# The sixth expert's rows by quarter gathers and VectorE, and a smaller margin in the plan of the searches

## The chip, the cores and the metric

The kernel runs on one core of one Trainium2 chip. Its engines are TensorE (PE, with its weight loads as PEld), VectorE (DVE), ScalarE (ACT), GpSimd (POOL), which issues gathers, scatters and accumulating transfers here, and SyncE (SP), which issues the plain loads. The metric is the time of one execution on the device in microseconds; lower is better.

## The reference

The input is first put through an attention with decay (8 batches of 8 heads, 576 positions of 64 values): scores are scaled, multiplied by a decay that falls with the distance, and used without a softmax. Its output, 4608 rows of 512 values, goes to eight experts of two layers. The rows are shared out by a greedy rule over all gate values at once:

```python
logits = x @ w_gate                      # 4608 rows, 8 experts
order = np.argsort(-logits.flatten())
for idx in order:
    tok, e = (int(idx) // E, int(idx) % E)
    if assigned[tok] >= 0 or counts[e] >= cap:   # cap = 576
        continue
    assigned[tok] = e
    counts[e] += 1
...
for e in range(E):
    mask = assigned == e
    h = np.maximum(x[mask] @ w1[e], 0.0)         # 512 -> 1024
    out[mask] = h @ w2[e]                        # 1024 -> 512
```

Each expert ends up with exactly 576 rows.

## The kernel before

The attention comes first and leaves its rows in DRAM (`xd`), with the gate values in SBUF. Then the experts are computed one after another, in the order in which they fill up. Their numbers here are places in that order, from 0; the sixth is expert 5.

**The two layers.** An expert's 576 rows stand in five tiles of 128 (the last has 64). Every product is made in two parts, a high part rounded to a narrower format and the low rest, so that three matmuls stand for one: high by high, low by high, high by low. `l1` (line 1066) runs 16 groups of 12 matmuls into PSUM, in columns of 256 and 320; `l2` (line 1109) runs four tiles of 24 matmuls, in triplets, and the half tile of 16, in pairs. Weights come in 512 KB pieces by SP into four `raw` buffers; `conv` makes a piece's high part on ScalarE (line 955) and its low part in one of two ways: for `e < PIECES` by a negated copy on ScalarE (line 964) and an accumulating transfer that GpSimd issues (line 965), for the others by subtractions on VectorE (line 958).

**The rows of an expert.** For `e < PIECES`, five gathers of 128 rows (line 998), then in `transposes` four TensorE transposes for each of the five tiles (line 1030), a copy by ScalarE and a subtraction by VectorE (lines 1032 and 1033). For the others, 18 quarter gathers of 128 x 128 values (line 986), five stream transposes on VectorE into `xz` (line 1014), a copy by ScalarE (line 1016) and a subtraction by VectorE (line 1017). The weights of layer 1 are then read from an array with another order of rows (`in_w1n`), since the quarters place the values otherwise.

**The searches.** Which rows belong to the next expert is found while the present one is computed. `search` takes seven steps. In each, VectorE builds a table `G` (line 179), TensorE counts with nine small matmuls (line 355), and VectorE goes from the sums (`cs`, line 359) over a few tiny operations to the next digit. `members` follows (a scan into `sc`, line 414, `sm`, line 418, two small matmuls, lines 423 and 424, then lines 426 and 427), and then `listing`, which makes the list of row numbers: VectorE tables (lines 436 to 455), nine matmuls (line 461), for most experts one more (line 464), and the sums (line 469 on). For `p >= PIECES` the listing makes the quarters' numbers too (lines 478 to 482). `leave` takes the expert out of the choice.

**What sets the order.** Each engine runs its instructions in the order in which the program writes them, and waits by semaphores. The searches are generators that yield an assumed VectorE time and a TensorE time. `Mixer` keeps an assumed clock for TensorE (`t`, moved on by `adv` behind the layers' matmuls) and one for VectorE (`v`); a step's TensorE part is written behind the first layer matmuls at which `t` has reached `v + 150`, where `v` had the step's VectorE time times `slack` added:

```python
d, s.pe = next(s.side)
s.vec(d * s.slack)
s.ready = s.v + 150
...
while not hold and s.side is not None and s.ready <= s.t:
    s.step()
```

So the plan decides how many layer matmuls stand between two steps, and the hardware waits where the plan was too tight. Gathers are written as soon as a list is ready, quarter gathers 1300 ns of assumed time apart, and the transposes of an expert when `t` has passed an assumed arrival (`state['arrives']`).

Of the kernel before, what the change touches and what calls it, by code (L numbers as in the profile page):

```python
# [19 lines left out]
NP, HP, NB = 4, 4, 9  # L20
N, DM, E, FF = 4608, 512, 8, 1024
SLACK = 1.0
PIECES = 6

def consts_np():
    h = np.arange(H); g = (1.0 - 2.0 ** (-5.0 - h)).astype(np.float64)
# [61 lines left out]
class Route:  # L88
# [341 lines left out]
    def listing(s, p):  # L430
# [43 lines left out]
        if early:  # L474
            s.room(cn)
        if p >= PIECES:
            s.quarter = pool.tile([128, 20], I32, name="quarter", bufs=2)
# [423 lines left out]
def moe(tc, nc, P, R, xd, w1_d, w2_d, out, mix):  # L901
# [11 lines left out]

    def phases():
        for p in range(E):
            mix.slack = 1.0 if p < 2 else 1.2 if p < 4 else 1.35
            if p < E - 1:
                yield from (R.search() if p else R.search_first())
                regs[p] = nc.sync.value_load(R.e[0:1, 0:1], min_val=0, max_val=E - 1)
            state['listing'] = p  # L920
            yield from R.members(p)
            if p == E - 1:
                regs[p] = nc.sync.value_load(R.e[0:1, 0:1], min_val=0, max_val=E - 1)
            yield from R.listing(p)
            found.append(R.idx)
            if p >= PIECES:
                quarters[p] = R.quarter
            if p == 0:
                yield 0, 0
            if p < E - 1:  # L930
                yield from R.leave(p)

    def dma_pump():

        while state['dma'] < min(state['conv'] + 4, 8*E):
            e, k = divmod(state['dma'], 8)
            if e not in regs or state['dma'] >= state['most']:
                return
            t = P['raw']()
            src = ((w1_d[0] if e < PIECES else w1_d[1]) if k < 4 else w2_d)  # L940
            nc.sync.dma_start(t, src[bass.ds(regs[e], 1), :, (k % 4)*1024:(k % 4)*1024+1024].rearrange("a p x -> (a p) x"))
            RAW[e, k] = t
            state['dma'] += 1

    def conv(fast=False):

        e, k = divmod(state['conv'], 8)
        if state['dma'] <= state['conv']:
            mix.drain(lambda: e in regs)
            dma_pump()  # L950
        raw = RAW.pop((e, k))
        nm = "w1" if k < 4 else "w2"
        hi = P['w'].tile([128, 1024], F32R, name=nm + "h", bufs=4)
        lo = P['w'].tile([128, 1024], F32R, name=nm + "l", bufs=4)
        A.activation(hi, raw, AF.Copy)
        if e >= PIECES:
            for x in (slice(0, 512), slice(512, 1024)):
                V.tensor_tensor(lo[:, x], raw[:, x], hi[:, x].bitcast(F32), op=ALU.subtract)
                mix.vec(690)
        elif fast:  # L960
            for x in (slice(0, 512), slice(512, 1024)):
                lows.append(lambda x=x: V.tensor_tensor(lo[:, x], raw[:, x], hi[:, x].bitcast(F32), op=ALU.subtract))
        else:
            A.activation(lo, raw, AF.Copy, scale=-1.0)  # L964
            add = lambda: nc.gpsimd.dma_start(lo, raw, accum_op=ALU.add)  # L965
            if ready(0) and 0 not in XG:
                lows.append(add)
            else:
                add()
        (W1 if k < 4 else W2)[e, k % 4] = (hi, lo)  # L970
        state['conv'] += 1
        dma_pump()

    def gather(e, all=False):
        if e in XG or not ready(e):
            return
        if e >= PIECES:
            if e not in parts:
# [24 lines left out]
    def transposes(e):  # L1003
# [4 lines left out]
        XH[e], XL[e] = xh, xl  # L1008
        if e >= PIECES:
            low = []  # L1010
# [26 lines left out]
    def l1(e, tr):  # L1037
# [5 lines left out]
        for i, (f, s) in enumerate(order):  # L1043
# [36 lines left out]
            if i in ((2, 4, 7, 10) if e else (5, 7, 9, 11, 13)):  # L1080
                conv()
# [10 lines left out]
    def l2(e, hb):  # L1092
# [4 lines left out]
        for t in range(5) if e + 1 < E else (4, 0, 1, 2, 3):  # L1097
# [4 lines left out]
            for f in range(8):  # L1102
                wh, wl = [w[:, (f % 2)*512:(f % 2)*512+512] for w in W2[e, f // 2]]

                h = hb[:, f]
                for a, w in ((h[:, c], wh), (h[:, 640+128*t:768+128*t], wh), (h[:, c], wl)) if t < 4 else \
                        ((h[:, 512:640], wh), (h[:, c], wl)):
                    m = a.shape[1]
                    T.matmul(ps[:m], a, w, start=(k == 0), stop=(k == last), skip_group_check=True)  # L1109
                    k += 1  # L1110
                mix.adv(650)
                gather(e + 1)
                wait -= 1

                soon = state['listing'] == e + 1 and not ready(e + 1)
                if want and wait <= 0 and e + 1 in regs and not soon:
                    conv()
                    want, wait = want - 1, 6
                if late and not soon:
                    late.pop(0)()  # L1120
                if e + 1 in XG and e + 1 not in XH and mix.t > state['arrives']:
                    tr = transposes(e + 1)
                next(tr, None)
# [9 lines left out]
        for _ in range(want):  # L1133
            conv()
# [6 lines left out]
    def prepare():  # L1141
# [4 lines left out]
                                     in_offset=bass.IndirectOffsetOnAxis(ap=z[:, 0:1], axis=0))  # L1146

    mix.start(phases())

    def run():  # L1150
# [98 lines left out]
```

## Time and profile before

| what | value |
|---|---|
| three runs | 619.55, 617.11, 616.14 us, median 617.11 |
| profiled execution | 619.8 us, of it the span of the instructions 618.0 us |
| granted TensorE clock, mean over the span | 0.989 |
| PE busy | 596.2 us (96%) |
| PEld busy | 517.8 us (84%) |
| DVE busy | 431.5 us (70%) |
| ACT busy | 252.0 us (41%) |
| POOL busy | 244.1 us (39%) |

A share of busy time is a mean over the whole span. TensorE is the engine that is nearly always busy; where it isn't, the timeline tells in brackets how long it stood before an instruction and which engine released it. In such a row the first number is the start in us from the beginning of the span, the second the busy time, then come engine, line, operation, written and read tiles, shape and number of instructions. The start of the next row of the same engine tells what an instruction costs when others follow, since matmuls overlap.

### The profile page before, as it was taken

The page shows a single profiled execution, that of the slowest core. Times are in us where ns is not written, and L with a number is a line of the kernel's source. Part 1 is how long each engine was busy: PE and PEld are TensorE (multiplying, and loading weights), DVE is VectorE, ACT ScalarE, POOL GpSimd, SP SyncE. Part 2 cuts the span into 40 slices and gives each one's busy share as a digit, 9 for nine tenths or more (in the row PEclk, how much of TensorE's full clock was granted, in tenths as well). Part 3 has the DMA queues.
Part 4 walks back from the last instruction along what each step waited for, and adds up shares of the span by engine and source line. Part 5 has one row for each costly group of instructions (what it writes and reads, how often), then busy time and mean ns, then how long its engine had stood idle before and what let it go on. Part 6 is the DMA issues. An engine that isn't in the chain of part 4 may idle for free.

```text
span 618.0 us, 14880 instructions
## 1 busy us (share of the span) xinstructions
PE 596.2 (96%) x5768; PEld 517.8 (84%) x5768; DVE 431.5 (70%) x1511; ACT 252.0 (41%) x437; POOL 244.1 (39%) x313
## 2 busy tenths in 40 slices
PE   8899997998999999999999999999999999999995
PEld 5788786876599889888987998898889789989983
DVE  6747886988889888878885976688578665544400
ACT  2334332333455446453562555166335234433310
POOL 5787635504512261262242143223314658711011
PEclk9999997998999999999999999999999999999998
DMA  9999999864688599696988398569928743440010
GB/s 329 407 379 398 278 329 334 278 168 154 185 234 171 178 232 251 194 213 200 200 220 266 70 248 207 176 142 242 249 82 186 207 158 116 152 142 27 0 43 34
DMA packets 51224, 124.83 MB, mean 202 GB/s; under 512 B 7186, under 2 KB 22418, under 8 KB 51154
## 3 DMA queue, kind: packets, MB, share of 16 engines
q1 hardware_dynamic: 37906, 80.10, 37.3%
q0 software_dynamic: 13104, 43.53, 31.2%
q8 instruction: 45, 0.74, 0.5%
q10 hardware_dynamic: 144, 0.26, 0.1%
q14 instruction: 25, 0.20, 0.1%
HBM read 80.35 MB, written 18.87 MB: 161 GB/s over the span
## 4 chain that ended last, share of the span: by engine, by line
PE 72%; issue 11%; DMA 8%; DVE 4%; POOL 3%; SPq 0%; POOLq 0%; ACT 0%; DVEq 0%
PE ph L1066 29%; PE py L1109 25%; DMA vin<-in_vk 4%; PE sc L605 3%; PE px L649 3%; DMA xd<-raw 3%; PE pS L626 2%; PE r L355 2%; PE px L640 2%; PE pt L1030 2%; POOL out_y L1086 1%; PE warm L1201 1%; PE r L461 1%; DMA qin<-in_qk 1%; PE pT L681 1%
## 5 line engine op out<-in xcount | busy, mean ns | idle before, releaser
L1109 PE MATMUL py<-w2h,hb 128*128 128x512 f32 x576 | 187.3, 397 | 0.1
L1066 PE MATMUL ph<-xh,w1h 128*128 128x320 f32 (+1 forms) x512 | 151.9, 301 | 0.2 <-ACT xh L1032 0.2
L1066 PE MATMUL ph<-xl,w1h 128*128 128x320 f32 (+1 forms) x512 | 149.2, 296 | 0.0
L1066 PE MATMUL ph<-xh,w1l 128*128 128x320 f32 (+1 forms) x512 | 149.0, 296 | 0.0
L1109 PE MATMUL py<-w2l,hb 128*128 128x512 f32 (+1 forms) x320 | 125.3, 391 | 0.1
L1109 PEld LDWEIGHTS py<-w2h,hb 128*128 128x128 f32 x576 | 104.5, 188 | 21.9 <-issue 0.3
L1066 PEld LDWEIGHTS ph<-xh,w1h 128*128 128x128 f32 x512 | 96.0, 189 | 1.3 <-ACT xh L1032 0.7
L1066 PEld LDWEIGHTS ph<-xl,w1h 128*128 128x128 f32 x512 | 96.2, 190 | 0.3
L1066 PEld LDWEIGHTS ph<-xh,w1l 128*128 128x128 f32 x512 | 96.0, 189 | 0.0
L1070 ACT ACTIVATE hb<-ph 128x256 fp32r<-128x256 f32 (+1 forms) x128 | 51.9, 408 | 105.2 <-PE ph L1066 98.9
L1086 POOL DMA_INDIRECT out_y<-yt,idx x40 | 40.3, 1008 | 129.4 <-ACT yt L1126 72.8
L1075 DVE SCALAR_TENSOR_TENSOR hb<-ph,hb 128x256 fp32r<-128x256 f32 (+1 forms) x192 | 57.7, 350 | 28.6 <-ACT hb L1070 24.3
L1109 PEld LDWEIGHTS py<-w2l,hb 128*128 128x128 f32 (+1 forms) x320 | 56.7, 177 | 13.5 <-issue 0.5
L590 POOL TENSOR_TENSOR qin<-qin,cst 128x512 f32<-128x512 f32 (+1 forms) x48 | 47.0, 1005 | 42.6 <-DMA qin<-in_qk 38.6
L1126 ACT ACTIVATE yt<-py 128x512 f32<-128x512 f32 x32 | 19.1, 597 | 98.2 <-PE py L1109 65.3
L629 ACT ACTIVATE st<-pS,cst 128x128 f32<-128x128 f32 x64 | 23.5, 367 | 83.6 <-PE pS L626 83.6
L614 DVE TENSOR_TENSOR am<-sc,cst 128x1024 f32<-128x1024 f32 x32 | 39.1, 1221 | 25.7 <-PE sc L605 25.7
L965 POOL DMA_DIRECT2D w2l<-raw x24 | 21.7, 904 | 73.4 <-ACT w2l L964 39.4
L998 POOL DMA_INDIRECT xg<-xd,idx x30 | 30.0, 1000 | 42.7 <-DVE room L496 16.1
L986 POOL DMA_INDIRECT xg<-xd,quarter x36 | 36.1, 1002 | 11.1 <-issue 8.5
L605 PE MATMUL sc<-qin,kin 64*128 64x128 f32 x512 | 38.3, 290 | 1.7 <-POOL ks L595 1.5
L965 POOL DMA_DIRECT2D w1l<-raw x23 | 21.1, 932 | 41.9 <-ACT w1l L964 34.6
(195 smaller groups left out, 944.6 us busy)
## 6 DMA issues: line engine op xcount, KB each, us to landing
raw<-in_w SPq DMA_DIRECT2D x56, 512.0 KB, 5.2
w2l<-raw POOLq DMA_DIRECT2D x24, 512.0 KB
w1l<-raw POOLq DMA_DIRECT2D x23, 512.0 KB
qin<-in_qk SPq DMA_DIRECT2D x14, 576.0 KB, 8.7
kin<-in_qk SPq DMA_DIRECT2D x14, 576.0 KB
vin<-in_vk SPq DMA_DIRECT2D x14, 576.0 KB
nin<-in_vk SPq DMA_DIRECT2D x14, 512.0 KB, 11.3
xd<-raw SPq DMA_DIRECT2D x36, 128.0 KB, 6.2
```

What stands on the lines that cost most here:

```text
L590: nc.gpsimd.tensor_tensor(x, x, e[:, None, :n].to_broadcast([128, (b-a)//n, n]), op=ALU.mult)
L605: nc.tensor.matmul(t[:, h, 128*j:128*j+128], blk(k, 4*g+j)[r], blk(q, 4*g+j)[r], start=(j == 0), stop=True, skip_group_check=True)
L614: nc.vector.tensor_tensor(a, SC[u, g].rearrange("p h (j q) -> p h j q", q=128), m1[:, u % HP, :, None, :].to_broadcast([128, 2, 4, 128]), ...
L629: nc.scalar.activation(s, p, AF.Copy, scale=ss[:, u % HP, c:c+1])
L965: add = lambda: nc.gpsimd.dma_start(lo, raw, accum_op=ALU.add)
L986: nc.gpsimd.indirect_dma_start(out=t[:, k, :], out_offset=None, in_=xq[:, :], in_offset=bass.IndirectOffsetOnAxis(ap=quarters[e][:, v:v+1] ...
L998: nc.gpsimd.indirect_dma_start(out=xg[:n, j, :], out_offset=None, in_=xd[:, :], in_offset=bass.IndirectOffsetOnAxis(ap=found[e][:n, j:j+1] ...
L1066: T.matmul(ps, w, x, start=(k == 0), stop=(k == 11))
L1070: A.activation(hb[:, f, c], ps, AF.Relu)
L1075: V.scalar_tensor_tensor(hb[:, f, to+a:to+b], ps[:, a:b], 0.0, hb[:, f, 256*s+a:256*s+b].bitcast(F32), op0=ALU.max, op1=ALU.subtract)
L1086: st = nc.gpsimd.indirect_dma_start(out=out[:, :], out_offset=bass.IndirectOffsetOnAxis(ap=found[e][:n, t:t+1], axis=0), in_=y[:n], in_off ...
L1109: T.matmul(ps[:m], a, w, start=(k == 0), stop=(k == last), skip_group_check=True)
```

## The change

Two constants and one factor. `PIECES` falls from 6 to 5, so that expert 5's rows come by quarter gathers and are turned by VectorE, its listing makes the quarters' numbers, and its layer 1 reads `in_w1n`. A new constant `BYDVE = 6` keeps the low parts of its weights as they were, by accumulating transfers. And the searches for experts 4 and later are planned with a slack of 1.2 in place of 1.35. Every line behind line 23 is one further down.

```diff
--- before.py
+++ after.py
@@ -20,7 +20,8 @@
 NP, HP, NB = 4, 4, 9
 N, DM, E, FF = 4608, 512, 8, 1024
 SLACK = 1.0
-PIECES = 6
+PIECES = 5
+BYDVE = 6
 
 def consts_np():
     h = np.arange(H); g = (1.0 - 2.0 ** (-5.0 - h)).astype(np.float64)
@@ -913,7 +914,7 @@
 
     def phases():
         for p in range(E):
-            mix.slack = 1.0 if p < 2 else 1.2 if p < 4 else 1.35
+            mix.slack = 1.0 if p < 2 else 1.2
             if p < E - 1:
                 yield from (R.search() if p else R.search_first())
                 regs[p] = nc.sync.value_load(R.e[0:1, 0:1], min_val=0, max_val=E - 1)
@@ -953,7 +954,7 @@
         hi = P['w'].tile([128, 1024], F32R, name=nm + "h", bufs=4)
         lo = P['w'].tile([128, 1024], F32R, name=nm + "l", bufs=4)
         A.activation(hi, raw, AF.Copy)
-        if e >= PIECES:
+        if e >= BYDVE:
             for x in (slice(0, 512), slice(512, 1024)):
                 V.tensor_tensor(lo[:, x], raw[:, x], hi[:, x].bitcast(F32), op=ALU.subtract)
                 mix.vec(690)
```

The order of the instructions moves with it. The first place is TensorE at the end of expert 2's layer 2, where the half tile is computed and expert 3's layer 1 begins; `r<-oh,G` are the matmuls of a search step, of which the last of nine is shown. Before:

```order
L1109 MATMUL py<-w2l,hb 64x512
L1109 MATMUL py<-w2h,hb 128x512
L1109 MATMUL py<-w2l,hb 64x512
L355 LDWEIGHTS G
L355 MATMUL r<-oh,G 128x32
...
L355 MATMUL r<-oh,G 128x32
L1066 MATMUL ph<-xh,w1h 128x256
L1066 MATMUL ph<-xl,w1h 128x256
L1066 MATMUL ph<-xh,w1l 128x256
```

In the changed kernel, from the end of one step to the beginning of the next:

```order
L356 MATMUL r<-oh,G 128x32
L1110 MATMUL py<-w2h,hb 128x512 x2
L1110 MATMUL py<-w2l,hb 128x512
L1110 MATMUL py<-w2h,hb 128x512
L1110 MATMUL py<-w2l,hb 64x512
L1110 MATMUL py<-w2h,hb 128x512
L1110 MATMUL py<-w2l,hb 64x512
L1110 MATMUL py<-w2h,hb 128x512
L1110 MATMUL py<-w2l,hb 64x512
L1110 MATMUL py<-w2h,hb 128x512
L1110 MATMUL py<-w2l,hb 64x512
L356 LDWEIGHTS G
```

Before, the last five pairs of the half tile stand ahead of a step that is followed by layer 1. Now one triplet and four pairs stand between two steps, and four more pairs with six matmuls of layer 1 follow up to the next one. At the end of expert 3's layer 2 a triplet and six pairs now stand between the last step and the members' matmuls.

The second place is VectorE between the members' last operation before TensorE's part (`sm<-sm`) and the first table of the listing for expert 6, whose matmuls TensorE has to wait for. Before, in expert 5's layer 1 (`hb<-ph,hb` are results of the layer):

```order
L418 SCALAR_TENSOR_TENSOR sm<-sm 128x36
L1075 SCALAR_TENSOR_TENSOR hb<-ph,hb 128x256
L1075 SCALAR_TENSOR_TENSOR hb<-ph,hb 128x64
L1075 SCALAR_TENSOR_TENSOR hb<-ph,hb 128x256 x2
L1075 SCALAR_TENSOR_TENSOR hb<-ph,hb 128x64
L426 SCALAR_TENSOR_TENSOR sm<-mem,r,sm 128x36
L427 SCALAR_TENSOR_TENSOR pq<-mem,r,sm 128x36
L436 TENSOR_SCALAR hb_7033<-pq 128x36
L438 SCALAR_TENSOR_TENSOR lb<-pq,hb_7033 128x72
```

In the changed kernel, in expert 4's layer 2:

```order
L419 SCALAR_TENSOR_TENSOR sm<-sm 128x36
L1015 STREAM_TRANSPOSE xz<-xg 128x512
L1018 TENSOR_TENSOR xl<-xz,xh 128x4x128
L1015 STREAM_TRANSPOSE xz<-xg 128x512
L1018 TENSOR_TENSOR xl<-xz,xh 128x4x128
L1015 STREAM_TRANSPOSE xz<-xg 128x512
L1018 TENSOR_TENSOR xl<-xz,xh 128x4x128
L1015 STREAM_TRANSPOSE xz<-xg 128x4x64
L1018 TENSOR_TENSOR xl<-xz,xh 128x4x128
L1018 TENSOR_TENSOR xl<-xz,xh 128x4x64
L427 SCALAR_TENSOR_TENSOR sm<-mem,r,sm 128x36
L428 SCALAR_TENSOR_TENSOR pq<-mem,r,sm 128x36
```

The search for expert 6 now ends within expert 4, and four of the five stream transposes of expert 5's rows (`xz`) and all five subtractions (`xl`) stand ahead of the operations that the listing needs; the first transpose stands one step earlier. On TensorE, 45 matmuls of full tiles and 12 of the half tile, and the members' two, stand between the search's last step and this listing's matmuls.

The third place is GpSimd in the stage of expert 4, where `w2l` and `w1l` are the accumulating transfers of low parts and `out_y` the scatters of results. Before:

```order
L965 DMA w2l<-raw 128x1024 x3
L998 DMA xg<-xd,idx 128x512 x4
L998 DMA xg<-xd,idx 64x512
L965 DMA w2l<-raw 128x1024
L965 DMA w1l<-raw 128x1024 x2
L1085 MEMSET spacer_2308 1x1
L1086 DMA out_y<-yt,idx 4608x512
```

In the changed kernel:

```order
L987 DMA xg<-xd,quarter 128x128
L966 DMA w2l<-raw 128x1024
L987 DMA xg<-xd,quarter 128x128 x2
L966 DMA w2l<-raw 128x1024
L987 DMA xg<-xd,quarter 128x128 x3
L966 DMA w2l<-raw 128x1024
L987 DMA xg<-xd,quarter 128x128 x3
L966 DMA w2l<-raw 128x1024
L987 DMA xg<-xd,quarter 128x128 x6
L966 DMA w1l<-raw 128x1024
L987 DMA xg<-xd,quarter 128x128 x3
L966 DMA w1l<-raw 128x1024
```

Eighteen quarter gathers stand where five whole ones stood, and the low parts of the weights are spread between them: the fourth of w2 follows nine gathers.

## Rows read from the trace of the kernel before

**Rows 1.** The page's chain of work that ended last, shares of the span by line.

```profile
PE ph L1066 29%; PE py L1109 25%; DMA vin<-in_vk 4%; PE sc L605 3%; PE px L649 3%; DMA xd<-raw 3%; PE pS L626 2%; PE r L355 2%; PE px L640 2%; PE pt L1030 2%; POOL out_y L1086 1%; PE warm L1201 1%; PE r L461 1%; DMA qin<-in_qk 1%; PE pT L68
```

**Rows 2.** Busy time by stretch: us, PE, PEld, DVE, ACT, POOL, PEclk, DMA share, GB/s.

```profile
397.57:454.11 56.54, 56.54 (x401) 49.69 (x400) 41.94 (x181) 26.69 (x42) 17.44 (x23) 1.00 0.75 191
```

**Rows 3.** Timeline of PE, the transposes of expert 5: start us, us, line, out<-in.

```profile
425.38 0.51 PE L1030 MATMUL pt<-ident,xg 128*128 128x128 f32 x4
...
430.20 0.74 PE L1109 MATMUL py<-w2h,hb 128*128 128x512 f32 x2
```

**Rows 4.** Timeline of PE, layer-2 triplets with nothing between.

```profile
435.48 0.62 PE L1109 MATMUL py<-w2h,hb 128*128 128x512 f32 x2
...
436.16 0.62 PE L1109 MATMUL py<-w2h,hb 128*128 128x512 f32 x2
```

**Rows 5.** Timeline of DVE, rows of expert 6 turned and split.

```profile
498.48 1.30 DVE L1014 STREAM_TRANSPOSE xz<-xg 128x512 f32<-128x512 f32 x2
...
505.05 0.45 DVE L1014 STREAM_TRANSPOSE xz<-xg 128x256 f32<-128x256 f32 x1 [1.47 <-DMA xg<-xd,quarter]
505.42 0.99 DVE L1017 TENSOR_TENSOR xl<-xz,xh 128x512 fp32r<-128x512 f32 x2
```

**Rows 6.** Timeline of PE, half tile of expert 4 and a search step.

```profile
450.08 0.39 PE L1109 MATMUL py<-w2h,hb 128*128 128x512 f32 x1
...
452.39 0.39 PE L355 MATMUL r<-oh,G 128*128 128x32 bf16 x9
...
452.95 0.40 PE L1109 MATMUL py<-w2l,hb 128*64 128x512 f32 x1
```

**Rows 7.** Timeline of PE, two short steps of the searches.

```profile
281.29 0.39 PE L355 MATMUL r<-oh,G 128*128 128x32 bf16 x9
...
283.45 0.28 PE L1066 MATMUL ph<-xh,w1h 128*128 128x256 f32 x1
...
284.03 0.28 PE L1066 MATMUL ph<-xh,w1l 128*128 128x256 f32 x1
284.50 0.39 PE L355 MATMUL r<-oh,G 128*128 128x32 bf16 x9 [0.18 <-DVE G L179]
...
337.48 0.39 PE L355 MATMUL r<-oh,G 128*128 128x32 bf16 x9
...
340.67 0.39 PE L355 MATMUL r<-oh,G 128*128 128x32 bf16 x9
```

**Rows 8.** Timeline of DVE, first operation behind the matmuls of 281.29.

```profile
281.71 0.15 DVE L359 SCALAR_TENSOR_TENSOR cs<-room,r 32x8 f32<-32x8 f32 x1 [0.41 <-PE r L355]
```

**Rows 9.** Timeline of DVE, last step's end, members and listing of expert 6.

```profile
456.51 0.14 DVE L359 SCALAR_TENSOR_TENSOR cs<-room,r 32x8 f32<-32x8 f32 x1
...
460.01 0.31 DVE L414 TENSOR_TENSOR_SCAN sc<-mem 128x72 bf16<-128x72 f32 x1
...
460.62 0.20 DVE L418 SCALAR_TENSOR_TENSOR sm<-sm 128x36 f32<-128x36 f32 x1
...
462.36 0.25 DVE L426 SCALAR_TENSOR_TENSOR sm<-mem,r,sm 128x36 f32<-128x36 f32 x1
...
465.86 0.52 DVE L455 TENSOR_TENSOR rh<-rh,cc 128x720 bf16<-128x720 bf16 x1
```

**Rows 10.** Timeline of all engines at a hold in expert 5's layer 2.

```profile
492.42 0.19 PEld L1109 LDWEIGHTS py<-w2l,hb 128*128 128x128 f32 x1 [0.54 <-issue]
...
492.52 0.60 ACT L1126 ACTIVATE yt<-py 128x512 f32<-128x512 f32 x1 [9.04 <-issue]
...
492.60 0.19 DVE L469 COPY lo<-r 32x40 f32<-32x40 f32 x1 [4.85 <-remote]
```

**Rows 11.** View of line 986: duration ns min/median/max, first and last start.

```profile
L986 POOL DMA_INDIRECT xg<-xd,quarter x36: 940/972/1347, 473.3 to 536.7; - x36
```

**Rows 12.** Timelines of POOL and SP: low-part transfer, next load into its buffer.

```profile
441.23 0.87 POOL L965 DMA_DIRECT2D w1l<-raw  x1 [0.86 <-ACT w1l L964]
...
449.31 0.33 SPq L941 DMA_DIRECT2D raw<-in_w  x1
```

## The prediction

> **What bounds the kernel now.** Three views were read, in this order. The chain that ended last says where the end comes from: its first two lines are TensorE's matmuls of the experts' two layers, 29% and 25% of it [rows 1]. The busy time by stretch then says whether TensorE has room there: through the whole stage of expert 4, the stage that the change alters most, it is busy for all of 56.54 us, at the full granted clock, VectorE for 41.94 [rows 2]. So in this part a matmul taken off TensorE is worth its time, and a wait of TensorE costs its time; no other engine decides. The timelines, last, give what each costs.
>
> **The gain: the transposes of expert 5.** Five groups of four transposes go from TensorE. From the first of the last such set to the layer matmul behind the fifth are 430.20 - 425.38 = 4.82 us, and four triplets of layer matmuls lie in it [rows 3]. A plain triplet takes 436.16 - 435.48 = 0.68 [rows 4]. So the five groups cost 4.82 - 4 x 0.68 = 2.10 us of TensorE.
>
> **What VectorE gets instead.** Five stream transposes of expert 5's rows, and eight small operations more in its listing. In the rows of expert 6, which already goes this way, the five transposes and five subtractions run from 498.48 to 506.41, 1.47 of it waiting for the last gather [rows 5]. VectorE has 14.6 us free in a stage [rows 2], so its sum fits; what matters is what stands behind these operations at one moment. TensorE works in a written order: if a step of the search is placed before VectorE has its table, TensorE stands. The smaller margin places steps closer. I therefore compared, for each step, the matmuls between two groups of nine with the time that VectorE needs.
>
> Prices on TensorE. A layer-2 matmul of tiles 0 to 3 takes 0.68 / 3 = 0.227; of the half tile, with ten of them in between, (452.39 - 450.08) / 10 = 0.231; the nine matmuls of a step (452.95 - 452.39) - 0.23 = 0.33, with what they delay behind them [rows 6]. A layer-1 matmul of 256 columns takes (284.03 - 283.45) / 5 = 0.116 [rows 7].
>
> The chain between two steps. Where TensorE had too little between them, the next nine began 3.21 (281.29 to 284.50, released by VectorE's table) and 3.19 us later (337.48 to 340.67) [rows 7]; I take 3.20 as the least that a step with sixteen digits can take. From the nine matmuls to the first operation on their sum are 281.71 - 281.29 = 0.42 [rows 7, 8]. From there to the end of the scan that the members' matmuls read are 460.32 - 456.51 = 3.81, and two short operations later, about 0.5, VectorE is free. The listing's operations from the members' sums to its last table take 466.38 - 462.36 = 4.02 [rows 9].
>
> **New waits, place by place.**
> - End of expert 2's layer 2, between steps 5 and 6 of the search: three matmuls of a full tile and eight of the half tile, 0.68 + 1.85 + 0.33 = 2.86, against 3.20: 0.34.
> - Steps 6 to 7, across into expert 3's layer 1: eight of the half tile and six of layer 1, 1.85 + 0.70 + 0.33 = 2.88: 0.32.
> - End of expert 3's layer 2, from step 7 to the members: 0.68 + 12 x 0.231 + 0.33 = 3.78, against 0.42 + 3.81 + 0.06 = 4.29: 0.51 (the 0.06 is from a table's end to the matmuls, the estimate that the label in [rows 7] leaves room for).
> - End of expert 4's layer 2, from step 7 to the listing. VectorE now has, between the scan and the listing, four stream transposes and five subtractions. By expert 6's rows they take 506.41 - 498.48 - 1.47 - 0.65 = 5.8 (without the wait and without one transpose, which comes earlier). VectorE: 0.42 + 4.3 + 5.8 + 4.0 + 0.1 = 14.6. TensorE: 45 x 0.227 + 12 x 0.231 + 0.33 and some 0.1 for the members = 13.4. Wait: 1.2. Queued behind the waiting listing matmuls are the last four of layer 2 and the whole of expert 5's layer 1. The wait could be 0.7 if the pause of 0.48 in [rows 5] does not come back, and 2.7 if the wait of 1.47 for the last gather does.
>
> Together 0.34 + 0.32 + 0.51 + 1.2 = 2.37. The kernel before has two short steps that now go elsewhere, 337.48 to 340.67 and its like an expert later: 3.19 - (12 x 0.231 + 0.33) = 0.09 each, 0.18. New waits net: 2.19.
>
> **Parts that I cost at nothing.** The searches, members and listings that move from expert 5's stage to those of 3 and 4 keep their counts, so on TensorE they are a zero sum. The remaining steps have fifteen full-tile matmuls between them, 15 x 0.227 + 0.33 = 3.74, above 3.20. The eight small operations delay the first gather by what the same eight take for expert 6, under 2 us, ahead of an expert whose rows are wanted a whole layer later; that cover gone, the 1.47 of [rows 5] would return, and is in the range. The low parts of expert 5's weights still go by transfers. What GpSimd gets, eighteen narrow gathers in place of five, is a rival below.
>
> **Sum.** 2.19 - 2.10 = +0.1 us, against the profiled execution of 619.8 (span 618.0): 619.9. The three runs have the median 617.11, 2.7 under that execution, so the forecast is 617.2 us: no change. A difference under 0.5%, 3.1 us, can't be told from none here.
>
> **Rivals.**
> 1. The waits do not come, since a floor taken from two steps of other stages need not hold where VectorE has fewer results of the layers to handle. For it: at 281.29 VectorE took up the sum 0.42 later, which includes such work if any was in its way. Against it: the two steps agree within 0.02. And the hold near the end of the gathers in expert 5's stage may vanish: TensorE's weight load stood 0.54 there [rows 10]. Time: 617.1 - 2.1 - 0.5 = 614.5. Chance 0.13.
> 2. A hold like that one falls into expert 4. At 492 VectorE came 4.85 us late to sums that lay ready and ScalarE 9.04, released by nothing that the profile names [rows 10], while narrow gathers were being issued. Expert 5's stage had few steps then, and TensorE lost only 0.5. Now narrow gathers run through expert 4, where a step has 3.74 - 3.20 = 0.54 to spare: a hold of 4.85 would cost 4.85 - 0.54 = 4.3. Time: 617.2 + 4.3 = 621.5, slower than before; it decides from a hold of about 3.5 us on. For it: both engines stood at once. Against: of 36 narrow gathers' surroundings only one place shows it. Chance 0.17.
> 3. GpSimd comes late. In expert 4 the last low part of w2 stands behind nine narrow gathers, before behind five wide ones. A narrow gather is issued in 972 ns, the longest took 1347 [rows 11]. Nine of the longest: 9 x 0.375 = 3.4 us late, and the buffer of such a transfer was free 8.1 us after its issue (441.23 to 449.31) [rows 12]; nothing shows how much of that TensorE has in hand. Between 0 and 3.4 I take 3.0, as the margin after nine gathers looks small: 620.2. Chance 0.10. On this rival the Trainium skill has a rule (SBUF — State Buffer, in "SBUF: two separate sides"): while VectorE runs an operation in a two-port mode, GpSimd can't write the descriptors of its transfers until that operation ends. It speaks against putting more of them beside a busier VectorE. By the rule gathers would stretch wherever VectorE copies or scales; the trace hardly shows that, with a median of 972 beside a minimum of 940, so by the rows the sum stands as above, and by the rule it would be near this rival's 620.2.
>
> **How the numbers follow.** The forecast has 0.55; the three rivals 0.13, 0.17 and 0.10; 0.05 is left for small waits that I have not listed. The case itself reaches from 616.1 (half of the waits) to 618.9 (1.47 for the last gather, with the small ones). The range that holds 8 in 10 goes from rival 1 to rival 3, with part of rival 2: 614.4 to 621.2. Faster by over 0.5% means under 614.0: a third of rival 1 and a part of the unlisted, 0.07. Slower means over 620.2: four fifths of rival 2, four tenths of rival 3, 0.18. The rest, 0.75, is no change.
>
> **What would show it.** Right: no transposes by TensorE in expert 4's layer 2, some 2.1 us shorter for that; TensorE standing about 0.3, 0.3, 0.5 and 1.2 us at the four places, each released by VectorE (a table, the scan, the listing's last table); narrow gathers at about 1.27 us each. Wrong: the listing at the end of expert 4 waiting under 0.5 or over 3; a stand of over 3 us on VectorE or ScalarE that nothing named releases; a layer-2 matmul waiting for a low part of w2.

## The result, and the profile after

The changed kernel took 619.82 us (median of 13 runs, 618.18 to 624.31), the kernel before 616.21 us in 13 runs beside it. The ratio is 1.0055, with a 95% interval of 1.0035 to 1.0075: slower by about 3.4 us. The forecast was 617.2 us, 0.1 above the kernel before, with a range of 614.4 to 621.2. The time lies in the range, but by the forecast's own measure of 3.1 us this is slower and not "no change". The sum missed some 3.3 us, and this is where they are.

The two profiled executions can't be compared by their spans, 617.9 and 618.0. The program is the same up to the experts, yet the first matmul of expert 0's layer 1 came at 167.57 us in one and 163.94 in the other; in the profiles of all ten kernels run here it came between 162.8 and 167.6. Timelines of TensorE, the kernel before and then the changed one (start us, busy us, engine, line, operation):

```profile
167.57 0.39 PE L1066 MATMUL ph<-xh,w1h 128*128 128x256 f32 x1 [0.21 <-ACT xh L1032]
```

```profile
163.94 0.39 PE L1067 MATMUL ph<-xh,w1h 128*128 128x256 f32 x1 [0.21 <-ACT xh L1033]
```

So I measure two pieces: from that matmul to the start of the last scatter, which I call the stage, and from there to the end of the span. Timelines of GpSimd, with the span in the head line, before and after:

```profile
core 0 of [0], span 618.0 us
611.29 0.96 POOL L1086 DMA_INDIRECT out_y<-yt,idx  x1 [4.44 <-ACT yt L1126]
```

```profile
core 0 of [0], span 617.9 us
610.13 0.96 POOL L1087 DMA_INDIRECT out_y<-yt,idx  x1 [4.44 <-ACT yt L1127]
```

The stage grew from 611.29 - 167.57 = 443.72 to 610.13 - 163.94 = 446.19, by 2.47 us. The end grew from 618.0 - 611.29 = 6.71 to 7.77, by 1.06. Together 3.53, near the 3.4 of the runs. The spans are taken to the hundredth: 618.00 and 617.90. The stage of before holds some 0.5 us of pauses near 491 that belong to this one execution; a second trace of the same instructions, under "The end of the program", has a stage of 443.14.

The stage of expert 4 shows it in one row (columns as in [rows 2]), changed kernel:

```profile
395.49:453.21 57.72, 55.67 (x390) 48.70 (x389) 49.81 (x205) 26.99 (x42) 31.65 (x36) 1.00 0.75 185
```

TensorE now stands 2.05 us here, where it stood for none of 56.54 [rows 2], and VectorE is busy 49.81 in place of 41.94. These are the places in the stage where TensorE waits longer than before, changed kernel, in order of time; the number ahead of the arrow is the part that the view counts as idle:

```profile
335.52 0.24 PE L356 MATMUL r<-oh,G 128*128 128x32 bf16 x3 [0.17 <-DVE G L180]
...
338.71 0.27 PE L356 MATMUL r<-oh,G 128*128 128x32 bf16 x4
...
394.43 0.18 PE L424 MATMUL r<-sc,cb 128*128 128x2 bf16 x1 [0.36 <-DVE sc L415]
...
410.75 0.31 PE L356 MATMUL r<-oh,G 128*128 128x32 bf16 x6 [0.46 <-DVE G L180]
...
414.93 0.31 PE L1067 MATMUL ph<-xh,w1l 128*128 128x320 f32 x1
415.38 0.29 PE L356 MATMUL r<-oh,G 128*128 128x32 bf16 x5
...
449.65 0.40 PE L1110 MATMUL py<-w2l,hb 128*64 128x512 f32 x1
451.49 0.32 PE L462 MATMUL r<-rh,G 128*128 128x160 bf16 x2 [1.45 <-DVE rh L456]
...
462.71 0.16 PE L424 MATMUL r<-sc,cb 128*128 128x2 bf16 x1 [0.63 <-DVE sc L415]
...
485.81 0.50 PE L1110 MATMUL py<-w2l,hb 128*128 128x512 f32 x1 [0.67 <-DMA w2l<-raw]
```

The table counts from the start of the matmul ahead to the start of the one that waits, less what the matmul ahead costs: 0.23 in layer 2, 0.15 or 0.12 in layer 1 for 320 or 256 columns. So for the listing it is 451.49 - 449.65 - 0.23 = 1.61. The steps at 338.71 and 415.38 carry no label in the view.

| place | forecast us | after us |
|---|---|---|
| end of expert 2, steps 5 to 6 (335.52) | 0.34 | 0.34 |
| across to expert 3, steps 6 to 7 (338.71) | 0.32 | 0.31 |
| end of expert 3, members (394.43) | 0.51 | 0.53 |
| expert 4, layer 1, first two steps (410.75, 415.38) | 0 | 0.59 + 0.30 |
| end of expert 4, listing (451.49) | 1.2 | 1.61 |
| expert 5, layer 1, last members (462.71) | 0 | 0.80 |
| expert 5, layer 2, a low part of w2 (485.81) | 0 (rival 3: in expert 4) | 0.83 |

That is 5.31. Less the forecast's 2.10 for the transposes and 0.18 for before's own short steps, and less the 0.5 of the pauses near 491, 2.53 are left; the stage grew by 2.47.

VectorE's rows tell why TensorE stands in expert 4's layer 1, and what is in the wait for the listing. Changed kernel, timeline of VectorE in expert 4's layer 1 and at the end of its layer 2:

```profile
402.39 0.17 DVE L479 TENSOR_SCALAR lo<-lo 32x40 f32<-32x40 f32 x1
...
403.95 0.17 DVE L507 TENSOR_SCALAR eb<-es 128x8 f32<-128x8 f32 x1
...
409.94 0.76 DVE L180 TENSOR_TENSOR G<-ct,v 128x1152 bf16<-128x1152 bf16 x1
...
446.19 1.03 DVE L1018 TENSOR_TENSOR xl<-xz,xh 128x512 fp32r<-128x512 f32 x2 [0.74 <-ACT xh L1017]
...
450.91 0.52 DVE L456 TENSOR_TENSOR rh<-rh,cc 128x720 bf16<-128x720 bf16 x1
```

From the copies of the list at 400.31 to the table's end at 410.70, VectorE works without a pause. The quarters' numbers take 403.95 - 402.39 = 1.56 of that, and the table is what TensorE waits for at 410.75. At 446.19 VectorE stands 0.74 for ScalarE, which had taken two weight conversions (`w1h`, `w1l`) ahead of the copy that VectorE needs:

```profile
443.65 1.04 ACT L956 ACTIVATE w1h<-raw 128x1024 fp32r<-128x1024 f32 x1
444.60 1.04 ACT L965 ACTIVATE w1l<-raw 128x1024 fp32r<-128x1024 f32 x1
445.55 0.92 ACT L1017 ACTIVATE xh<-xz 128x512 fp32r<-128x512 f32 x2
```

The last place in the table is GpSimd's, in expert 5. Its queue stands behind a scatter of expert 4's half tile, whose last operation VectorE could not take up before 459.42. From there on GpSimd issues without a pause, and eleven quarter gathers for expert 6 stand ahead of the fourth low part of w2, where the kernel before had three. So that part is issued at 478.76, 7.0 us before TensorE can go on at 485.81:

```profile
460.37 0.90 POOL L1087 DMA_INDIRECT out_y<-yt,idx  x1 [10.58 <-DVE yt L1130]
...
478.76 1.02 POOL L966 DMA_DIRECT2D w2l<-raw  x1
```

One gather takes about as long as before; minimum, median and longest are to be compared with [rows 11].

```profile
L987 POOL DMA_INDIRECT xg<-xd,quarter x54: 942/975/1442, 404.7 to 535.0; - x54
```

### The profile page after: what moved, and what is told of

The parts are those of the page before. It is cut to its first block, busy times and chain, and to the rows that moved or that the text cites. A ratio compares the mean times of both kernels' runs of the same rounds, so it can differ in the third digit from the quotient of the medians.

```text
span 617.9 us, 14857 instructions
## 1 busy us (share of the span) xinstructions
PE 593.3 (96%) x5746; PEld 514.5 (83%) x5748; DVE 435.3 (70%) x1524; ACT 253.1 (41%) x437; POOL 259.6 (42%) x326
## 4 chain that ended last, share of the span: by engine, by line
PE 61%; issue 13%; DVE 11%; DMA 9%; POOL 4%; ACT 1%; SPq 1%; POOLq 0%; DVEq 0%
PE ph L1067 22%; PE py L1110 21%; PE sc L606 4%; PE px L650 3%; DMA vin<-in_vk 3%; DMA w2l<-raw 2%; PE pS L627 2%; PE px L641 2%; DMA xd<-raw 2%; PE r L356 2%; POOL xg L987 2%; POOL out_y L1087 1%; PE pt L1031 1%; DVE am L615 1%; PE pT L682 1%
## 5 line engine op out<-in xcount | busy, mean ns | idle before, releaser
L987 POOL DMA_INDIRECT xg<-xd,quarter x54 | 55.0, 1018 | 18.0 <-issue 12.7
L999 POOL DMA_INDIRECT xg<-xd,idx x25 | 25.0, 1002 | 40.2 <-DVE room L497 14.8
```

What stands on the lines that cost most here:

```text
L987: nc.gpsimd.indirect_dma_start(out=t[:, k, :], out_offset=None, in_=xq[:, :], in_offset=bass.IndirectOffsetOnAxis(ap=quarters[e][:, v:v+1] ...
L999: nc.gpsimd.indirect_dma_start(out=xg[:n, j, :], out_offset=None, in_=xd[:, :], in_offset=bass.IndirectOffsetOnAxis(ap=found[e][:n, j:j+1] ...
```

## Experiments

**The rows alone.** The old margin with the rows by VectorE:

```diff
-            mix.slack = 1.0 if p < 2 else 1.2
+            mix.slack = 1.0 if p < 2 else 1.2 if p < 4 else 1.35
```

> The changed kernel with the old margin (slack 1.35 from expert 4 on): expert 5's rows still come by quarter gathers and VectorE. Theory A (the tighter plan makes TensorE wait for VectorE, and the moved transposes are a clean gain): the 2.1 us of TensorE's transposes are gone, the stands at the ends of layer 2 of experts 2 and 3 and the 1.6 us ahead of the listing in expert 4 are gone, so 2 to 2.6 us under the kernel before, a ratio of 0.996 to 0.997. Theory B (the quarter gathers and VectorE's extra work cost by themselves, GpSimd too): ratio 1.002 or more, with stands of TensorE on a low part or on VectorE in the stages of experts 4 and 5.

Measured: 620.89 us, ratio 1.0088 (1.0059 to 1.0117). Theory A fell; theory B's number came, but TensorE waits for no low part and for no table. Expert 4's layer 2 is 29.67 - 27.47 = 2.2 us shorter than before, as the absence of the transposes wants, and the stands of the plan are gone. But expert 5's layer 1 takes 32.77 us, before 26.84. Expert 4's layer 2 before; then, in this run, that layer, expert 5's layer 1, and a stretch of it (columns as in [rows 2]):

```profile
424.44:454.11 29.67, 29.67 (x189) 23.07 (x188) 18.40 (x81) 12.95 (x18) 7.90 (x13) 1.00 0.86 219
```

```profile
420.79:448.26 27.47, 27.47 (x168) 21.45 (x167) 19.73 (x86) 12.07 (x16) 21.66 (x25) 1.00 0.82 204
448.26:481.03 32.77, 29.93 (x215) 29.37 (x213) 24.52 (x100) 15.11 (x27) 8.57 (x10) 0.90 0.60 148
452.13:458.96 6.83, 6.28 (x32) 6.02 (x33) 3.33 (x13) 1.83 (x4) 0.91 (x1) 0.50 0.24 70
```

The layer is longer for two reasons. TensorE stands for rows, some 3.0 us from start to start. And from 452.13 to 458.96, while this stand still lasts and behind it, its granted clock is 0.50, the lower of its two levels (1.2 in place of 2.4 GHz): matmuls of 256 columns then start 0.21 us apart, before 0.116 [rows 7]. The 6.28 us that it is busy in that stretch would be some 3.5 at the rate of the full clock, so this costs about 2.8 us more, by an estimate from these rows. In the stages of the kernel before and of the changed kernel the clock is 1.00. Timelines of TensorE, GpSimd and VectorE:

```profile
449.56 0.28 PE L1067 MATMUL ph<-xh,w1l 128*128 128x256 f32 x1
452.68 0.64 PE L1067 MATMUL ph<-xh,w1h 128*128 128x320 f32 x1 [2.84 <-ACT xh L1017]
...
456.24 0.41 PE L1067 MATMUL ph<-xh,w1h 128*128 128x256 f32 x1
456.45 0.42 PE L1067 MATMUL ph<-xl,w1h 128*128 128x256 f32 x1
```

```profile
414.43 1.19 POOL L987 DMA_INDIRECT xg<-xd,quarter  x1 [3.57 <-DVE gone L508]
...
444.84 1.05 POOL L987 DMA_INDIRECT xg<-xd,quarter  x1 [0.30 <-issue]
```

```profile
449.11 0.15 DVE L360 SCALAR_TENSOR_TENSOR cs<-room,r 32x8 f32<-32x8 f32 x1
...
451.74 0.44 DVE L1015 STREAM_TRANSPOSE xz<-xg 128x256 f32<-128x256 f32 x1
```

The 18 gathers, with other work of GpSimd between them, take from 414.43 to 445.89, and expert 5's layer 1 begins at 448.26. Five whole gathers took some 6 us in the kernel before. The view shows no wait of VectorE for a gather; the last transpose (451.74) stands behind a search step that VectorE begins at 449.11, since the plan writes the transposes by the time at which the gathers were written. So the quarter gathers need a list that is ready early, and the old margin makes it late: the first gather comes 20.5 us after the start of expert 4 here and 9.2 in the changed kernel. The smaller margin is thus not a second change beside the first but its condition.

**Two experts' rows.** The same with `PIECES = 4`.

> The old margin (1.35), and the rows of experts 4 and 5 both by quarter gathers and VectorE (PIECES = 4). Theory A: two sets of TensorE transposes are gone, 4.2 us, and no step is placed too early: ratio 0.992 to 0.994, the fastest so far. Theory B: GpSimd with one more set of 18 gathers delivers low parts late, or VectorE falls behind the steps in experts 3 and 4: ratio 0.999 or more.

Measured: 634.85 us, ratio 1.0299 (1.0269 to 1.0330). Far off theory A, and the same cause in experts 4, 5 and 6. TensorE's waits for rows from 300 to 520 us (us in total, times, longest):

```profile
PE ph L1067 <- ACT xh L1017: 9.0, 3, 3.3
PE ph L1067 <- DVE xl L1018: 2.8, 3, 1.1
```

The view has 0.3 us for one more wait and none for a low part. Here too the granted clock falls to 0.50 during or just behind these stands, at 397.79 and 459.23 for 6.82 us and at 520.66 for 3.42. The first stretch (columns as in [rows 2]):

```profile
397.79:404.61 6.82, 5.64 (x22) 5.47 (x23) 3.15 (x8) 1.83 (x4) 0.90 (x1) 0.50 0.09 19
```

**The plan alone.** The kernel before with the smaller margin.

```diff
-            mix.slack = 1.0 if p < 2 else 1.2 if p < 4 else 1.35
+            mix.slack = 1.0 if p < 2 else 1.2
```

> The kernel before with only the smaller margin (slack 1.2 from expert 2 on), expert 5's rows still turned by TensorE. Theory A: the stands of about 0.3, 0.3 and 0.5 us at the ends of layer 2 of experts 2 and 3 appear, one of some 0.9 ahead of the members of the last expert in expert 5's layer 1, against 0.2 of before's own: 1.5 to 2.2 us slower than before, ratio 1.0025 to 1.0035; no stand ahead of the listing in expert 4, since no rows stand in front of it on VectorE. Theory B: within 0.5 us of before, ratio 0.999 to 1.001.

Measured: 617.30 us, ratio 1.0031 (1.0008 to 1.0054); the stage is 445.50, 1.78 longer. Theory A holds: the stands at the ends of experts 2 and 3 are there, none stands ahead of a listing, and the one for the last members is 1.5 from start to start instead of 0.9. TensorE's waits from 300 to 520 us:

```profile
PE r L423 <- DVE sc L414: 1.7, 2, 1.4
PE r L355 <- DVE G L179: 0.3, 2, 0.2
```

The margin alone costs 1.8 us of the stage, then; together with the rows on VectorE it costs the 2.5 and the 2.1 that the transposes give back. No stand in expert 4's layer 1 is among these waits, so those of the changed kernel do not come of the margin alone.

**The planner told of the quarters' operations.**

```diff
-            yield (5000 if p == 1 else 4300), 0
+            yield (5000 if p == 1 else 4300 + 1570*(p >= PIECES)), 0
```

> The changed kernel with the planner told of the 1.57 us that a listing with quarters takes VectorE longer (the assumed time behind a listing 5870 in place of 4300 ns for experts 5 and later). Theory A: the two stands in expert 4's layer 1 (0.59 and 0.30 us) and the one ahead of the last members (0.80) go, the one ahead of the listing for expert 6 stays at 1.5 to 2: 1.3 to 1.8 us under the changed kernel, ratio to before about 1.002. Theory B: those stands come from VectorE being held up by its neighbours, and come back at the new places: the changed kernel's ratio of about 1.004 to 1.0055.

Measured: 617.36 us, ratio 1.0033 (1.0014 to 1.0052). Theory A holds, with more gained in the stage than it said. The stage is 443.56, 2.6 shorter than the changed kernel's and, without the pauses near 491, 0.4 longer than before's; by the trace mainly the longer end is left. The two stands in expert 4's layer 1, the one ahead of the last members and the one for a low part are gone, more than expected. What stands ahead of the listing moved to the members ahead of it, 1.2 and 0.6 from start to start. TensorE's waits from 300 to 520 us:

```profile
PE r L424 <- DVE sc L415: 1.4, 2, 1.0
PE r L462 <- DVE rh L456: 0.4, 1, 0.4
PE r L356 <- DVE G L180: 0.2, 1, 0.2
```

**The end of the program.** The kernel before and 13 quarter gathers more, into a tile that nothing reads, between the scatters of expert 6 and 7:

```diff
+        spare = P["w"].tile([128, 4, 128], F32, name="spare")
+        for k in range(13):
+            v = (0, 5, 10, 15)[k % 4]
+            nc.gpsimd.indirect_dma_start(out=spare[:, k % 4, :], out_offset=None, in_=xq[:, :],
+                                         in_offset=bass.IndirectOffsetOnAxis(ap=quarters[E - 2][:, v:v+1], axis=0))
```

> The kernel before with 13 quarter gathers more, into a tile that nothing reads, written on GpSimd between the scatters of expert 6 and those of expert 7, where GpSimd has nothing else to do. Theory C (the end of the program grows with the number of transfers that GpSimd has issued, not with where they stand): from the start of the last scatter to the end of the span 6.7 us become 7.8, as in the changed kernel, with TensorE's stages unchanged; about 1.0 us slower, ratio 1.0015 to 1.002. Theory D (the longer end comes from what the changed kernel does late, such as the quarters of expert 5): the end stays at 6.7 us and the ratio at 0.999 to 1.001.

Measured: 617.27 us, ratio 1.0033 (1.0015 to 1.0050), by its interval in line with the 1.0 us of theory C. Its last scatter and span:

```profile
core 0 of [0], span 614.4 us
606.65 0.96 POOL L1086 DMA_INDIRECT out_y<-yt,idx  x1 [4.44 <-ACT yt L1126]
```

The end, 614.425 - 606.654 = 7.77 us by the trace, is that of the changed kernel, without its change. Theory D is out. In passing: expert 5's layer 2 took 26.45 us here, 27.09 in the first profile of before, with the same instructions up to there, and the stage 443.14. The hold of [rows 10] was there in one of two executions.

**A margin between the two.** The changed kernel, the planner told as above, and

```diff
-            mix.slack = 1.0 if p < 2 else 1.2
+            mix.slack = 1.0 if p < 2 else 1.2 if p < 4 else 1.25
```

> The changed kernel with a margin between the two (slack 1.25 from expert 4 on) and the planner told of the 1.57 us that a listing with quarters takes VectorE longer. Theory A2 (the rows' move saves 2.1 us of TensorE if two things hold: steps not closer than VectorE's chain, and the list ready early enough for the 18 gathers to land before expert 5): the list for expert 5 is written at layer-1 matmul 66 of expert 4, in place of 111 in the run with the old margin, so no stand for the rows; the steps have at least 12 matmuls between them, so stands of at most 0.1 us each: TensorE's stages 1.7 to 2.1 us shorter than before, the end 1.05 longer, 0.6 to 1.1 us under the kernel before, ratio 0.998 to 0.999. Theory B: stands of over 1 us in the stages of experts 4 and 5 also here, ratio 1.002 or more.

Measured: 614.22 us, ratio 0.9984 (0.9963 to 1.0004), as theory A2 had it. The view of waits lists none for TensorE from 300 to 520 us. The stages of experts 4 and 5, layer by layer (columns as in [rows 2]):

```profile
393.06:419.90 26.84, 26.84 (x214) 26.59 (x213) 24.47 (x109) 13.97 (x24) 13.17 (x14) 1.00 0.60 140
419.90:447.30 27.40, 27.40 (x168) 21.37 (x167) 20.70 (x79) 13.08 (x18) 18.02 (x23) 1.00 0.93 236
447.30:474.08 26.78, 26.78 (x213) 26.59 (x209) 23.31 (x100) 13.86 (x24) 11.85 (x12) 1.00 0.69 165
474.08:500.33 26.25, 26.25 (x124) 21.13 (x122) 16.82 (x44) 9.34 (x14) 15.46 (x20) 1.00 0.59 187
```

The stage is 440.80 us, 2.92 under the kernel before: 2.1 of transposes, 0.5 of the pauses that were in that one execution, the rest small. The end is 7.77. Its interval just reaches 1, so that it beats the kernel before is likely and not shown; that it beats the changed kernel is plain from the two ratios, 0.9984 and 1.0055.

**The same plan with the rows on TensorE** (`PIECES = 6` in the run above).

> The same plan (1.25, planner told), with expert 5's rows still gathered whole and turned by TensorE (PIECES = 6). Theory A2: TensorE's stages within 0.5 us of before's, the end unchanged: ratio 0.999 to 1.0015, and the difference to the run with 1.25 and quarter gathers is what the move of the rows is worth when nothing waits, 2.1 - 1.05 = 1.0 us. Theory B: this one is faster than the run with 1.25 and quarter gathers.

Measured: 616.51 us, ratio 1.0004 (0.9987 to 1.0022); stage 443.52, end 6.67. By the two traces the rows' move is worth 443.52 - 440.80 = 2.72 of the stage, of which 0.75 is a stand of this plan ahead of the members in expert 4, less 1.10 at the end. Of the whole time this is not shown, as the intervals of the two ratios overlap.

**Fewer transfers.** The run with 1.25, and `BYDVE = 5`.

> The run with margin 1.25 and the planner told, and in addition the low parts of expert 5's eight weight pieces by subtractions on VectorE (BYDVE = 5), so that GpSimd issues eight accumulating transfers fewer (159 in place of 167). Theory C (the end of the program grows with every transfer that GpSimd issues, whatever its kind): the time from the start of the last scatter to the end of the span is 7.77 - 8 x 0.082 = 7.1 us. Theory C2 (only gathers count): it stays at 7.8 us. TensorE's stages: sixteen subtractions of 0.69 us are 11 us more for VectorE in the stages of experts 4 and 5, of which it has over 12 free in each; Theory A2 expects stands of at most 0.5 us more in all, and a time from 0.8 us under to 0.3 over the run with 1.25 (ratio to before 0.997 to 0.999). The other view, that VectorE is the next bound there: stands of 2 us or more, ratio 1.001 or more.

Measured: 615.36 us, ratio 0.9986 (0.9967 to 1.0006). The end is 612.75 - 605.63 = 7.12, as theory C had it: accumulating transfers count like gathers.

```profile
core 0 of [0], span 612.8 us
605.63 0.96 POOL L1087 DMA_INDIRECT out_y<-yt,idx  x1 [4.44 <-ACT yt L1127]
```

But the stage is 442.59 in this trace, 1.8 longer than without this edit, near the 2 of the other view; the whole time can't be told from that of the run with 1.25 (0.9986 against 0.9984). TensorE now waits for ScalarE. TensorE's waits from 300 to 520 us:

```profile
PE py L1110 <- ACT yt L1127: 0.8, 1, 0.8
PE ph L1067 <- ACT hb L1071: 0.5, 1, 0.5
```

The first of these is VectorE's doing, by the timeline of ScalarE. The copy `yt` that TensorE needs stands behind a copy of rows that waited 3.64 us for the third stream transpose:

```profile
443.05 0.63 ACT L1017 ACTIVATE xh<-xz 128x512 fp32r<-128x512 f32 x1 [3.64 <-DVE xz L1015]
443.59 0.58 ACT L1127 ACTIVATE yt<-py 128x512 f32<-128x512 f32 x1
```

The expectation gave VectorE over 12 us free in each stage. By the rows of the run with 1.25 it had 26.84 - 24.47 + 27.40 - 20.70 = 9.07 in expert 4's. Why ScalarE is late at the second wait stays open.

## Why the prediction came out as it did

The time lies in the range, but not by the merit of the sum. The sum gave no change, its own case ended at 618.9, and the part of the range above that stood there for rivals 2 and 3. Nearly all of the measured 3.4 us is what the sum had at nothing: 1.69 us of stands behind VectorE's chain, 0.83 for a low part and 1.06 at the end of the program.

**What bounds.** Right. A matmul off TensorE was worth its time: layer 2 of expert 4 fell by 2.2 us where nothing stood in it (the rows alone), against 2.10 forecast.

**The four new waits.** Right in place and size for three (0.34, 0.31 and 0.53 us against 0.34, 0.32 and 0.51), and in releaser for the two of them whose rows name one. So the floor of 3.20 us for a step holds: the steps at 338.71 and 335.52 came 3.19 and 3.20 us after the ones ahead. The fourth measured 1.61 against 1.2, inside its bounds of 0.7 to 2.7, with the pause for ScalarE at 0.74 where I had carried over 0.48.

**"Parts that I cost at nothing".** This is the step that failed. It said that what moves between stages is a zero sum and that the eight small operations only delay the gather. In the rows they stand in one line with the search's next table. The list, the quarters' numbers, the removal of the expert, the new choice, some results of the layer and the table are one unbroken chain on VectorE of 10.4 us (400.31 to 410.70), for which the plan counts too little by the quarters' 1.56. I had compared the matmuls between two steps within a search, and not from a listing to the first step behind it or to the next members. The first two stands are not there with the margin alone, and telling the planner of the quarters takes them away, with 2.6 us off the stage. These places cost 0.59 + 0.30 + 0.80 = 1.69.

**The end of the program.** Missing altogether, the second step that failed. The sum took what lies behind the last scatter as a constant; it holds 1.06 us more for 13 more transfers.

**Rival 1** (the waits do not come): refuted by the rows. Its other half, that the hold may vanish, came true, and this was luck: the hold was missing in a second execution of before's instructions too.

**Rival 2** (a hold in expert 4): did not come; in expert 4 the longest stand without a named releaser is 2.0 us, on ScalarE. In expert 5's layer 2 ScalarE has one of 4.14, which by its length is one of the prediction's signs of being wrong; TensorE waited for none of it.

**Rival 3** (GpSimd late): came in kind, for 0.83 us in place of 3.0, in expert 5 and not in expert 4, and with it the sign of being wrong that named a low part of w2. It did not come of longer gathers: their median is 975 ns against 972. The Trainium skill's rule on two-port operations (SBUF — State Buffer, "SBUF: two separate sides") thus made no time here that these numbers show. GpSimd was late since its queue had stood 10.6 us behind a scatter that waited for VectorE, and since eleven quarter gathers then stood ahead of the low part. With the planner told, eleven stand ahead of it too, but the scatter goes out 2.5 us into expert 5's layer 1 in place of 7.2, and TensorE does not stand.

**What I did not see as a rival:** that margin and rows hang together. Had I priced the two parts apart, the first would have been a gain of 2.1 with the listing where it was, and the run with the rows alone shows it 5.4 us slower than before. About half of that is the lower clock behind the stand, a cost that no rival had.

## What to carry to other kernels

Price a planned order from every producer to every consumer behind it, not only within one loop: a handful of tiny operations on a chain that the plan doesn't know of stops the engine that bounds. When a transfer is cut into many small ones, ask first when its input must be ready, since their issue alone can take most of a layer (18 x 1.27 = 23 us here, a layer 25 to 30); a margin that looks like slack may be what pays for that. Behind a long stand of the engine that bounds, read its granted clock: a view of waits shows the stand, not the slower matmuls that follow. And compare profiles by stages, with the time behind the last instruction as a stage of its own.

## What the runs showed of the hardware

The time from the start of the last scatter to the end of the span goes with the number of transfers that GpSimd has issued in the whole program: 6.63 to 6.71 us at 154 transfers (three traces), 7.12 at 159 (one), 7.77 to 7.81 at 167 (five), 8.79 at 180 (one), that is 0.08 us for each. Gathers and accumulating transfers count alike, and gathers that nothing reads, near the end of the program, count like those of expert 5. In that time no engine but GpSimd, with the 0.96 us of the scatter itself, has an instruction that the views count as work. What in the end of a program it is that counts them stays open.

TensorE's granted clock fell from 1.00 to 0.50 where TensorE had stood for rows: in the run with the rows alone for 6.83 us, near the end of a stand of 3.0 us, and three times with two experts' rows, for 6.82, 6.82 and 3.42 us. While it was 0.50, matmuls of 256 columns in layer 1 started 0.21 us apart in place of 0.12.
